# Value units 0 to 2 in the loop's common part, and one early projection instead of two

## The chip, the cores and the metric

The kernel runs on one core of one Trainium2 chip. The metric is the device time in microseconds (us); the median of several runs is quoted. The engines: TensorE does matmuls (PE in the profile; PEld is its weight load), VectorE is DVE, ScalarE is ACT, SyncE is SP and issues most of the loads.

## The reference, cut to what matters

One decoding step of a block: adaLN modulation, attention with a key and value cache, a squared-ReLU feed-forward part.

```python
B, Sq, D = 8, 1, 512;  Hq, Hkv, Sk, Dh = 32, 8, 8192, 128;  F = 1792
mod = (silu(c) @ w_mod)                       # six vectors sa, ca, ga, sb, cb, gb
h = layernorm(x) * (1 + ca) + sa
x = x + ga * A(h)      # q = h @ wq; p = softmax(q @ k_cache.T / sqrt(128)); o = p @ v_cache; o @ wo
h = layernorm(x) * (1 + cb) + sb
x = x + gb * B(h)      # relu(h @ w1 + b1)**2 @ w2 + b2
```

The two caches are 8 x 8 x 8192 x 128 bfloat16 values each, 134 MB. Each is read once. All else is about 15 MB.

## The kernel before

A batch is four key units and four value units. A unit is one load of 4 MB (two of the eight key-value heads), and four slots hold loaded units. The 64 units are loaded in order; the load of unit n + 4 waits until TensorE is done with unit n. The program of a batch is a hardware loop on TensorE, VectorE and ScalarE. Its body has a part "a" that all passes run, and a part "b" under a branch that the last pass skips. What only the last batch does stands after the loop ("post"). SyncE's program has no loop.

```python
def _looped(self, e, eng, passes):
    ...
    with nc.Fori(0, passes, engines=[pe], head_slot={pe: 0} if e == "tensor" else None) as i:
        for j, o in enumerate(self._part(e, (0, "a"))):
            self._emit(eng, o, first["a", j], seen)
        with eng.If(i < passes - 1):
            for j, o in enumerate(self._part(e, (0, "b"))):
                self._emit(eng, o, first["b", j], seen)
            ...                                  # wait for the counts, set the semaphores back
    for o in self._part(e, "post"):
        self._emit(eng, o, self._want(e, o, passes - 1), after)
```

The value units, with cuts (`...`). In the kernel before all four are in "b", and the last batch has its own copy of them after the loop:

```python
for b in range(B):
    lastb = b == B - 1
    Pg.at = (b, "a")
    ...                                          # keys: transposes, scores; softmax; pe_stream
    Pg.at = "post" if lastb else (b, "b")
    for p in range(NP):                          # value units 0..3
        if not lastu:
            for m in range(32):                  # 128 x 512 matmuls in four column groups
                ...                              # wait: this unit's load, the softmax
            osb = ...                            # VectorE copies 128 x 512 out of PSUM
            for i in range(4):                   # four SEL matmuls sum the groups;
                ...                              # the first of them releases the slot
            norm_last = ...                      # VectorE normalizes into oTn
            if lastb and p == 1:
                k_oP = early(0, 2, ...)          # gather: 16 matmuls and a copy
                ...                              # 14 bias matmuls (b1)
                project(0, 2, k_oP)              # 64 matmuls with wo
            if lastb and p == 2:
                k_oP = early(2, 3, [norm_last])
                ...                              # 4 bias matmuls (b2)
                project(2, 3, k_oP)              # 32 matmuls with wo
        else:                                    # the last unit of all, loaded in four chunks
            ...                                  # loads of B's weights w1 and w2 are issued
            for m in range(24): ...              # chunk 0 for m < 16, chunk 1 for the others
            direct(96, 112, 2, True, False)      # 16 narrow matmuls, chunk 2
            ...                                  # four SEL matmuls
            direct(112, 128, 3, False, True)     # 16 narrow matmuls, chunk 3
            ...                                  # normalize, the last 32 matmuls with wo
```

After the last value unit come the residual, the second layernorm, 56 matmuls with w1 and 56 with w2.

## Time and profile before

| | |
|---|---|
| time, median of 3 runs | 670.4 us (670.01 to 670.82) |
| bytes loaded | 283.65 MB, nearly all of it keys and values |
| TensorE, VectorE, ScalarE busy | 75%, 45%, 37% |
| DMA engines busy | 99.0% of 16 engines' span |

These lines are from the profile page of the kernel before: the span; the busy tenths of the DMA engines in 40 slices; one of the DMA queues with packets, MB and share (q8 carries instructions); and who stands in the chain of waits that ended last.

```profile
span 668.9 us, 16042 instructions
...
DMA  9999999999999999999999999999999999999996
...
q8 instruction: 11, 0.18, 0.1%
...
PE 54%; DMA 38%; DVE 3%; ACT 2%; SPq 2%; issue 1%
```

The DMA engines are busy 90% or more in 39 of 40 slices. The shares by engine of the last line are misleading on their own: where TensorE stands in the chain it is because it released a slot for a load that then waited in a queue (from issue to landing the 4 MB loads of keys and values took 33.6 and 27.8 us, where 4 MB at 431 GB/s are 9.7 us).

Windows of the kernel before: start and end, length, busy time of PE, PEld, DVE, ACT, POOL with instruction counts, then granted clock, DMA share, GB/s. First one batch's worth of the loop, then two of the last microseconds of loading.

```profile
553.00:631.00 78.00, 59.81 (x867) 41.43 (x866) 36.41 (x66) 29.74 (x36) 0.00 (x0) 0.87 1.00 431
...
663.00:664.00 1.00, 0.48 (x18) 0.48 (x19) 0.90 (x5) 0.00 (x0) 0.00 (x0) 0.50 0.14 55
664.00:665.00 1.00, 0.62 (x24) 0.53 (x21) 0.09 (x1) 0.00 (x0) 0.00 (x0) 0.50 0.07 29
```

In the loop the loads run at 431 to 432 GB/s with no gap, while TensorE is busy 60 of 78 us. (Six more such windows, from 85 us on, show the same.) At the end the share falls to 0.14, which is two of 16 engines, and 0.07, which is one: most DMA engines are done by about 662.5 us, but one or two are 1 to 2.5 us behind.

Timeline of TensorE in the last batch, kernel before (start, length, engine, line, what, and in brackets the idle time before it and what ended it):

```profile
643.04 1.78 PE L518 MATMUL PS<-oP,wo_sb 128*128 128x32 bf16 x64
645.20 1.91 PE L606 MATMUL PS<-ring,Pm 128*32 128x512 bf16 x32 [0.38 <-DMA ring<-in_A_v_cache_dram]
...
649.13 0.99 PE L518 MATMUL PS<-oP,wo_sb 128*128 128x32 bf16 x32 [0.19 <-DVE oP L512]
651.68 1.90 PE L665 MATMUL PS<-ring,Pm 128*32 128x512 bf16 x16 [1.56 <-DMA ring<-in_A_v_cache_dram]
...
664.92 1.01 PE L731 MATMUL PS<-hidT,ring 128*128 128x8 bf16 x24 [0.38 <-DMA ring<-in_B_w_dram]
```

64 projection matmuls (L518) while unit 2 is loading; unit 2 (L606) in 1.91 us at full clock (granted 1.00); 32 more projection matmuls; then the last unit's first 16 wide matmuls (L665), after a wait of 1.56 us for their chunk; at the end the w2 matmuls (L731), of which the last 24 wait 0.38 us for w2. The end of the chain of waits (start, length, what) says the same, a load of B's weights and then those matmuls:

```profile
649.87 15.01 DMA ring<-in_B_w_dram
...
664.92 0.59 PE PS L731 x16
```

### The profile page before, as it was taken

How to read it: one execution, taken by the hardware profiler on the slowest of the kernel's cores; microseconds unless marked ns; L12 is line 12 of the kernel's file. 1: busy time of each engine (PE TensorE's matmuls, PEld its weight loads, DVE VectorE, ACT ScalarE, POOL GpSimd, SP SyncE). 2: the span in 40 equal slices, each digit the busy share in tenths (PEclk: the TensorE clock that was granted, in tenths of full speed). 3: DMA queues.
4: the chain of work that ended last, by engine and by line, in shares of the span. 5: the costliest groups of instructions: out<-in, count | busy, mean ns of one | idle time of the engine just before them, and what ended most of it. 6: DMA issues, size and time to landing. Idle time of an engine off the chain costs nothing.

```text
span 668.9 us, 16042 instructions
## 1 busy us (share of the span) xinstructions
PE 501.8 (75%) x7348; PEld 347.5 (52%) x7348; DVE 301.2 (45%) x570; ACT 245.2 (37%) x289; POOL 17.8 (3%) x71
## 2 busy tenths in 40 slices
PE   3493974799539983699648996499836996399966
PEld 2382731676228751577317762287415773177644
DVE  1262741467216661367314672166503673156722
ACT  2151630466105650266304661066402653046600
POOL 7300000000000000000000000000000000000000
PEclk9696995799869996599957997699977999689995
DMA  9999999999999999999999999999999999999996
GB/s 373 436 402 435 421 429 435 433 431 427 437 433 433 425 433 435 433 429 429 435 431 435 427 433 435 431 425 433 435 433 431 427 437 433 431 427 433 435 410 246
DMA packets 12962, 283.88 MB, mean 424 GB/s; under 512 B 1266, under 2 KB 2323, under 8 KB 4372
## 3 DMA queue, kind: packets, MB, share of 16 engines
q1 hardware_dynamic: 12900, 283.65, 99.0%
q8 instruction: 11, 0.18, 0.1%
q10 hardware_dynamic: 48, 0.02, 0.0%
q14 instruction: 3, 0.02, 0.0%
HBM read 283.66 MB, written 0.01 MB: 424 GB/s over the span
## 4 chain that ended last, share of the span: by engine, by line
PE 54%; DMA 38%; DVE 3%; ACT 2%; SPq 2%; issue 1%
PE PS L467 36%; DMA ring<-in_A_k_cache_dram 36%; PE PS L484 9%; PE PS L564 3%; PE PS L606 2%; DMA ring<-in_B_w_dram 2%; PE PS L458 1%; SPq L648 1%; ACT KTb L472 1%; ACT P_sb L554 1%; DVE m L491 1%; DVE O_sb L612 1%; PE PS L585 0%; DVE Dm L545 0%; PE PS L616 0%
## 5 line engine op out<-in xcount | busy, mean ns | idle before, releaser
L472 ACT ACTIVATE KTb<-PS 128x1024 bf16<-128x1024 bf16 x192 | 196.7, 1024 | 344.3 <-PE PS L467 344.3
L467 PE MATMUL PS<-IDENT,ring 128*128 128x128 bf16 x4096 | 268.1, 228 | 51.3 <-DMA ring<-in_A_k_cache_dram 51.3
L467 PEld LDWEIGHTS PS<-IDENT,ring 128*128 128x128 bf16 x4096 | 247.5, 102 | 99.8 <-DMA ring<-in_A_k_cache_dram 52.9
L474 DVE COPY KTb<-PS 128x1024 bf16<-128x1024 bf16 x320 | 210.1, 688 | 145.1 <-PE PS L467 143.0
L606 PE MATMUL PS<-ring,Pm 128*32 128x512 bf16 x992 | 81.1, 485 | 61.9 <-DMA ring<-in_A_v_cache_dram 61.0
L612 DVE CAST O_sb<-PS 128x512 bf16<-128x512 f32 x31 | 21.4, 692 | 138.8 <-PE PS L606 138.8
L484 PE MATMUL PS<-KTb,Qb 128*32 128x512 bf16 x1024 | 78.8, 385 | 4.5 <-ACT KTb L472 4.5
L606 PEld LDWEIGHTS PS<-ring,Pm 128*32 128x32 bf16 x992 | 28.9, 115 | 99.3 <-DMA ring<-in_A_v_cache_dram 62.4
L458 PE MATMUL PS<-IDENT 128*128 128x512 bf16 x120 | 31.3, 380 | 0.0
L554 ACT ACTIVATE P_sb<-PS,negm 128x512 bf16<-128x512 f32 x32 | 21.6, 686 | 20.2 <-DVE negm L550 20.2
L616 PEld LDWEIGHTS PS<-SEL,O_sb 128*128 128x128 bf16 x124 | 5.3, 99 | 44.9 <-DVE O_sb L612 44.9
L616 PE MATMUL PS<-SEL,O_sb 128*128 128x8 bf16 x124 | 8.0, 170 | 24.8 <-DVE O_sb L612 24.8
L484 PEld LDWEIGHTS PS<-KTb,Qb 128*32 128x32 bf16 x1024 | 15.4, 94 | 21.1 <-ACT KTb L472 8.5
L579 DVE COPY Pm<-PS 64x512 bf16<-64x512 bf16 x48 | 19.5, 419 | 13.3 <-PE PS L564 12.3
L491 DVE TENSOR_REDUCE m<-PS 128x1 f32<-128x512 f32 x32 | 22.1, 689 | 6.6 <-PE PS L484 6.6
L564 PEld LDWEIGHTS PS<-IDENT,P_sb 128*64 128x64 bf16 x512 | 21.9, 109 | 5.2 <-ACT P_sb L554 5.2
L564 PE MATMUL PS<-IDENT,P_sb 128*64 128x128 bf16 x512 | 23.2, 222 | 1.2 <-ACT P_sb L554 1.2
L458 PEld LDWEIGHTS PS<-IDENT 128*128 128x128 bf16 x120 | 9.9, 103 | 10.8 <-issue 3.4
L623 DVE TENSOR_TENSOR oTn<-PS,rinv 128x8 f32 (+1 forms) x31 | 6.0, 194 | 14.0 <-PE PS L616 14.0
L472 ACT ACT_TABLE_LOAD x8 | 10.3, 1283 | 3.2 <-issue 3.2
L576 ACT ACTIVATE Pm<-PS 64x512 bf16<-64x512 bf16 x16 | 9.5, 592 | 3.1 <-PE PS L564 2.5
L393 PE MATMUL PS<-ring,KTb 128*32 128x512 bf16 x56 | 7.2, 627 | 3.6 <-DMA ring<-in_A_wq_dram 3.5
(126 smaller groups left out, 102.2 us busy)
## 6 DMA issues: line engine op xcount, KB each, us to landing
ring<-in_A_k_cache_dram SPq DMA_DIRECT2D x32, 4096.0 KB, 33.6
ring<-in_A_v_cache_dram SPq DMA_DIRECT2D x31, 4096.0 KB, 27.8
ring<-in_A_wq_dram SPq DMA_DIRECT2D x1, 4096.0 KB, 19.9
ring<-in_w_mod_dram SPq DMA_DIRECT2D x1, 3072.0 KB, 10.4
wo_sb<-in_A_wo_dram SPq DMA_DIRECT2D x1, 3072.0 KB, 46.1
ring<-in_A_v_cache_dram SPq DMA_DIRECT2D x1, 2048.0 KB, 24.2
ring<-in_B_w_dram SPq DMA_DIRECT2D x3, 512.0 KB, 18.4
ring<-in_B_w_dram SPq DMA_DIRECT2D x1, 1344.0 KB, 21.0
```

The costliest lines, as they stand in the source:

```text
L458: op("tensor", lambda e: e.matmul(bank(at).rearrange("p (a r) -> p a r", a=4), IDENT[:, :], rhs))
L467: t = op("tensor", lambda e, j=j, i=i: e.matmul(STG[j][:, i, :], src[:, 32 * k + 8 * j + i, :], IDENT[:, :], is_transpose=True), [loaded[n ...
L472: stg_free[j] = op("scalar", lambda e, j=j, dst=dst: e.activation(dst, STG[j], ACT.Copy), [t])
L474: stg_free[j] = op("vector", lambda e, j=j, dst=dst: e.tensor_copy(dst, STG[j]), [t])
L484: t = op("tensor", lambda e, hf=hf, q=q, rhs=rhs: e.matmul(PS[32 * q:32 * (q + 1), k, :], Qb[:, 2 * p + hf, :], rhs, start=(p == 0 and hf ...
L491: return op("vector", lambda e: e.tensor_reduce(m4[:, k:k + 1], bank(k), AX.X, ALU.max), [t])
L554: exps.append(op("scalar", lambda e, k=k: e.activation(P_sb[:, k, :], bank(k), ACT.Exp, bias=negm[:, 0:1], scale=inv_sqrt, accum_out=rs4[: ...
L564: t = op("tensor", lambda e, k=k, i=i, hf=hf, src=src: e.matmul(STG[k][64 * hf:64 * (hf + 1), i, :], src, IDENT[:, :], is_transpose=True, ...
L579: done.append(op("vector", lambda e, dst=dst, frm=frm: e.tensor_copy(dst, frm), [t, k_pm]))
L606: t = op("tensor", lambda e, p=p, m=m, cg=cg, vt=vt, Obank=Obank: e.matmul(Obank[32 * cg:32 * (cg + 1), :], lhs[:, p, 32 * m:32 * m + 32], ...
L612: t = op("vector", lambda e, osb=osb, Obank=Obank: e.tensor_copy(osb, Obank), [t])
L616: t = op("tensor", lambda e, i=i, osb=osb, oT_ps=oT_ps: e.matmul(oT_ps, osb[:, i * 128:(i + 1) * 128], SEL[:, i, :], start=(i == 0), stop= ...
```

## The change

Read from the diff, the intent is shorter code: units 0 to 2 of every batch move into the common part "a", so the last batch runs them in the loop and their second copy after the loop goes away. Only unit 3 stays under the branch. Since nothing of the last batch alone can stand in part "a", the early projection of the last batch, which was in two parts (after units 1 and 2), is done once after unit 2; the 14 b1 matmuls move in between the 16th and the 17th of unit 3's 24 wide matmuls. The program becomes shorter: counted in the compiled program, with two instructions for each matmul (weight load and matmul; the page of before counts 7348 of each), TensorE's code after the loop shrinks from 947 to 698 instructions, and the loop itself stays at 1747.

```diff
--- before.py
+++ after.py
@@ -500,19 +500,18 @@
         hT_ps = [bank(i)[:, 0:16 * 7].rearrange("p (f a b) -> p f a b", f=7, a=2) for i in range(2)]
         yT_ps = bank(2)[:, 0:KT * B].rearrange("p (k b) -> p k b", k=KT)
 
-        def early(q0, q1, deps):
-            nq = q1 - q0
-            pP = bank(6)[:, 64 * q0:64 * q1].rearrange("p (j g b) -> p j g b", j=4, g=2 * nq)
+        def early(deps):
+            pP = bank(6)[:, 0:192].rearrange("p (j g b) -> p j g b", j=4, g=6)
             for hl in range(REP):
                 for j in range(4):
                     t = op("tensor", lambda e, hl=hl, j=j: e.matmul(
                         pP[32 * hl:32 * (hl + 1), j, :, :].rearrange("p (q h) b -> p h q b", h=2),
-                        PERM[:, j, :], oTn_p[:, :, q0:q1, hl, :], start=True, stop=True,
+                        PERM[:, j, :], oTn_p[:, :, 0:3, hl, :], start=True, stop=True,
                         tile_position=(0, 32 * hl)), deps)
-            return op("vector", lambda e: e.tensor_copy(oP[:, :, 2 * q0:2 * q1, :], pP), [t])
-
-        def project(q0, q1, k_oP):
-            for g in range(2 * q0, 2 * q1):
+            return op("vector", lambda e: e.tensor_copy(oP[:], pP), [t])
+
+        def project(k_oP):
+            for g in range(6):
                 for j in range(4):
                     for k in range(KT):
                         op("tensor", lambda e, g=g, j=j, k=k: e.matmul(
@@ -594,8 +593,9 @@
             lhs = Pm[:, :, :, :].rearrange("p u t r -> p u (t r)")
             rinv_p = rinv[:].rearrange("p (h q r) -> p h q r", h=2, q=NP)
             oTn_p = oTn[:].rearrange("p (h q r) b -> p h q r b", h=2, q=NP)
-            Pg.at = "post" if lastb else (b, "b")
             for p in range(NP):
+                if p == NP - 1:
+                    Pg.at = "post" if lastb else (b, "b")
                 n = 2 * NP * b + NP + p
                 vt = tiles(n % NSLOT)
                 Obank = bank(p)
@@ -623,20 +623,13 @@
                     s_bank_free[p] = norm_last = op("vector", lambda e, p=p, b=b, oT_ps=oT_ps: e.tensor_tensor(
                         oTn_p[:, :, p, :, Pg.index(b)].rearrange("p h r o -> p h (r o)"), oT_ps.rearrange("p (h r) -> p h r", h=2), rinv_p[:, :, p, :], ALU.mult),
                         [t])
-                    if lastb and p == 1:
-                        k_oP = early(0, 2, [norm_last, k_all] + stg_free + hold)
-                        for f in range(FT):
-                            op("tensor", lambda e, f=f: e.matmul(
-                                hT_ps[f // 7][:, f % 7, 1, :], fcol(b1_row[:], f), ONE8[:, :],
-                                start=(f % 7 == 0), stop=False, skip_group_check=True), [d_b2, s_bank_free[f // 7]])
-                        project(0, 2, k_oP)
-                    if lastb and p == 2:
-                        k_oP = early(2, 3, [norm_last])
+                    if lastb and p == NP - 2:
+                        Pg.at = "post"
+                        project(early([norm_last, k_all] + stg_free + hold))
                         for k in range(KT):
                             op("tensor", lambda e, k=k: e.matmul(
                                 yT_ps[:, k, :], b2_row[:, k * 128:(k + 1) * 128], ONE8[:, :],
-                                start=(k == 0), stop=False, skip_group_check=True), [s_bank_free[2]])
-                        project(2, 3, k_oP)
+                                start=(k == 0), stop=False, skip_group_check=True), [d_b2, s_bank_free[2]])
                 else:
 
                     s0 = (n + 1) % NSLOT
@@ -667,6 +660,11 @@
                             vt[:, 4 * m:4 * m + 4, :], start=(m < 4), stop=(m >= 20),
                             tile_position=(0, 32 * cg)),
                             [loaded[n][0 if m < 16 else 1], k_rinv] + pmd[m // 8])
+                        if m == 15:
+                            for f in range(FT):
+                                op("tensor", lambda e, f=f: e.matmul(
+                                    hT_ps[f // 7][:, f % 7, 1, :], fcol(b1_row[:], f), ONE8[:, :],
+                                    start=(f % 7 == 0), stop=False, skip_group_check=True), [d_b2, s_bank_free[f // 7]])
                     osb = O_sb[:, 1, :]
                     t = op("vector", lambda e: e.tensor_copy(osb, bank(3)), [t])
                     direct(96, 112, 2, True, False)
```

## The prediction

> **What bounds the kernel now.** The DMA queue. Page part 2: the 16 DMA engines are 90% busy or more in 39 of 40 slices. In seven windows of 78 us (one batch each, from 85 to 631 us) the DMA share is 1.00 at 431 to 432 GB/s, while TensorE is busy about 60 of 78 us. The list of waits has TensorE standing 61.0 us (L606) and 51.3 us (L467) until loads land; issue to landing, 28 to 34 us (page part 6), is about three 4 MB loads of 9.7 us, so one is always queued. Nothing a compute engine does in the loop is on the critical path unless it delays a slot's release by more than about 18 us (estimate from that).

> **Inside the loop the change only moves the branch** from before value unit 0 to between units 2 and 3. There TensorE waits 5.0 to 5.6 us for unit 3 anyway (timeline). Loads, releases and instruction mix are unchanged. Expected: nothing.

> **The last batch changes.** Before (timeline, 636 to 669 us): units 0 and 1 end at 642.0; an early gather, 14 bias matmuls and 64 projection matmuls (1.78 us) fill the wait; unit 2 lands at 645.2 and runs at full clock (1.91 us); gather, 32 more projection matmuls (0.99 us) end at 650.1; unit 3's first chunk lands at 651.7. After: TensorE idles about 3 us from 642.0. After such a gap unit 2 took 3.02 to 3.60 us in batches 0 to 6, at granted clock 0.5. [...]
> Estimate: unit 2 ends near 648.5; copy 0.69, SEL 0.26, normalization 0.19; gather and copy about 0.8; 96 projection matmuls at 28 ns = 2.7 us; so TensorE is free at about 653.4, 1.7 us after unit 3's first chunk. Then 16 matmuls (1.9 us), 14 bias matmuls (0.6), 8 matmuls (1.04), partly using up waits of 0.68 and 0.36 us. Attention's last normalization moves from 657.4 to about 658.7 (+1.3 us; only +0.2 if unit 2 stays at full clock).

> **How much reaches the end.** The chain of waits ends in the load of B's second weight (landing at 664.9), not in attention. TensorE waits 0.42 us for the first weight at 660.1 and 0.38 us for the second at 664.9: slack of about 0.6 us. So +1.3 becomes about +0.6; +0.2 becomes 0.

> **Predicted: 670.9 us (before 670.4), 8 in 10 between 669.4 and 672.4.** Faster by over 2%: 0.005; within 2%: 0.985; slower: 0.01.

> **What would show it.** Loop windows: still 1.00 DMA share, about 431 GB/s. Timeline of the last batch: unit 2 after an idle gap of about 3 us, lasting 3.0 to 3.6 us; 96 projection matmuls in one run of about 2.7 us; unit 3's first matmul released by TensorE's own order, near 653.5, no longer by the load; bias matmuls between its 16th and 17th. End: the wait for the second weight shrinks or is gone.

> **What would make it wrong.** A stall at the jump out of the loop, now just ahead of the gather with only about 0.5 us to hide it ([...]this trace shows none at the old place). Another landing of the second weight, whose last packets straggle.

## The result, and the profile after

| | median us | runs |
|---|---|---|
| before | 670.2 | 4 (669.80 to 670.82) |
| after | 670.46 | 4 (669.77 to 670.78) |

The ratio is 1.0002, 95% interval 0.9984 to 1.0019: the same. A ratio here is the mean time of one kernel's runs over the mean of the other's of the same rounds, so it isn't quite the ratio of the medians. 670.46 us lies in the predicted range, 0.4 us from the predicted 670.9.

The page after, the same lines:

```profile
span 667.9 us, 16012 instructions
...
DMA  9999999999999999999999999999999999999996
...
q8 instruction: 10, 0.16, 0.1%
...
PE 54%; DMA 40%; DVE 3%; ACT 2%; issue 1%; SPq 0%; DVEq 0%
```

The windows after, the same stretches:

```profile
553.00:631.00 78.00, 59.95 (x867) 41.31 (x867) 36.41 (x66) 29.74 (x36) 0.00 (x0) 0.89 1.00 432
...
663.00:664.00 1.00, 0.86 (x32) 0.87 (x33) 0.64 (x4) 0.00 (x0) 0.00 (x0) 0.50 0.13 39
664.00:665.00 1.00, 0.93 (x30) 0.78 (x27) 0.03 (x1) 0.00 (x0) 0.00 (x0) 0.50 0.01 2
```

The loop is unchanged: share 1.00, 432 GB/s. At the end next to nothing is left between 664 and 665 us (0.01 of 16 engines, before 0.07). One 16 KB instruction load is gone (q8: 10 instead of 11).

TensorE's timeline of the last batch after:

```profile
644.74 2.70 PE L606 MATMUL PS<-ring,Pm 128*32 128x512 bf16 x32 [3.34 <-DMA ring<-in_A_v_cache_dram]
...
649.79 2.74 PE L517 MATMUL PS<-oP,wo_sb 128*128 128x32 bf16 x96 [0.51 <-DVE oP L511]
...
652.65 1.05 PE L658 MATMUL PS<-ring,Pm 128*32 128x512 bf16 x16
653.63 0.61 PE L665 MATMUL PS<-ONE,b_row 1*128 1x8 bf16 x14
654.16 0.40 PE L658 MATMUL PS<-ring,Pm 128*32 128x512 bf16 x3
655.20 0.59 PE L658 MATMUL PS<-ring,Pm 128*32 128x512 bf16 x5 [0.64 <-issue]
...
663.14 1.79 PE L729 MATMUL PS<-hidT,ring 128*128 128x8 bf16 x56 [0.97 <-DVE hidT L725]
```

- Unit 2 (L606 at 644.74) follows an idle wait of 3.34 us and takes 2.70 us (mean granted clock 0.68).
- The 96 projection matmuls (L517) are one run of 2.74 us.
- Unit 3's first matmul (L658 at 652.65) no longer waits for its load; it follows TensorE's own work. It runs at full clock: 16 matmuls in 1.05 us (granted 1.00), where before they took 1.90 (granted 0.50).
- Between the 19th and the 20th of unit 3's matmuls there is a pause of 0.64 us for which the profile names no releaser.
- The w2 matmuls (L729) show as one run of 56, but this view begins a new line only after an idle time of 0.15 us. w2 is loaded in four pieces, for 16, 16, 16 and 8 of these matmuls. In the trace's list of landings the last piece is there at 664.50 us, while the matmuls run, and the last 8 waited about 0.1 us for it: the 56 took 1.79 us, and 1.66 where nothing held them (after_again, below).

So the chain of waits, as the profile draws it, no longer passes through the load of w2, though the two end within 0.1 us of each other. It leaves the loads when unit 2 lands (the first of these two lines of the chain of waits ends at 644.70 us), and is TensorE's and VectorE's from then on, up to the w2 matmuls:

```profile
617.14 27.56 DMA ring<-in_A_v_cache_dram
...
663.14 1.80 PE PS L729 x56
```

The span of this one profile is 1.0 us shorter than that of before (667.9 and 668.9), but the times of the four runs don't differ. A second profile of each kernel was needed before any of this could be read.

### The profile page after: what moved, and what is told of

It reads as the page before. It is cut to its first block, busy times and chain, and to the rows that moved or that the text cites. A ratio compares the mean times of both kernels' runs of the same rounds, so it can differ in the third digit from the quotient of the medians.

```text
span 667.9 us, 16012 instructions
## 1 busy us (share of the span) xinstructions
PE 499.2 (75%) x7332; PEld 346.1 (52%) x7332; DVE 301.0 (45%) x569; ACT 245.1 (37%) x289; POOL 17.5 (3%) x71
## 4 chain that ended last, share of the span: by engine, by line
PE 54%; DMA 40%; DVE 3%; ACT 2%; issue 1%; SPq 0%; DVEq 0%
DMA ring<-in_A_k_cache_dram 36%; PE PS L467 35%; PE PS L484 9%; DMA ring<-in_A_v_cache_dram 4%; PE PS L563 3%; PE PS L606 2%; PE PS L458 1%; ACT KTb L472 1%; DVE O_sb L612 1%; ACT P_sb L553 1%; DVE m L491 1%; PE PS L517 0%; PE PS L584 0%; PE PS L658 0%; PE PS L729 0%
## 5 line engine op out<-in xcount | busy, mean ns | idle before, releaser
L467 PE MATMUL PS<-IDENT,ring 128*128 128x128 bf16 x4096 | 266.9, 228 | 51.3 <-DMA ring<-in_A_k_cache_dram 51.3
L467 PEld LDWEIGHTS PS<-IDENT,ring 128*128 128x128 bf16 x4096 | 246.2, 102 | 99.6 <-DMA ring<-in_A_k_cache_dram 52.5
L606 PE MATMUL PS<-ring,Pm 128*32 128x512 bf16 x992 | 82.2, 490 | 65.5 <-DMA ring<-in_A_v_cache_dram 64.6
L606 PEld LDWEIGHTS PS<-ring,Pm 128*32 128x32 bf16 x992 | 29.3, 115 | 103.4 <-DMA ring<-in_A_v_cache_dram 66.0
L484 PEld LDWEIGHTS PS<-KTb,Qb 128*32 128x32 bf16 x1024 | 15.5, 94 | 21.1 <-ACT KTb L472 8.5
L623 DVE TENSOR_TENSOR oTn<-PS,rinv 128x8 f32 x31 | 6.0, 194 | 14.3 <-PE PS L616 14.3
```

Source lines behind the costliest of these rows:

```text
L467: t = op("tensor", lambda e, j=j, i=i: e.matmul(STG[j][:, i, :], src[:, 32 * k + 8 * j + i, :], IDENT[:, :], is_transpose=True), [loaded[n ...
L484: t = op("tensor", lambda e, hf=hf, q=q, rhs=rhs: e.matmul(PS[32 * q:32 * (q + 1), k, :], Qb[:, 2 * p + hf, :], rhs, start=(p == 0 and hf ...
L606: t = op("tensor", lambda e, p=p, m=m, cg=cg, vt=vt, Obank=Obank: e.matmul(Obank[32 * cg:32 * (cg + 1), :], lhs[:, p, 32 * m:32 * m + 32], ...
```

## The experiments

My theory: the loads bound the kernel; in the loop the moved branch is hidden; in the last batch TensorE has a little slack against the load of w2, which swallows most of what its longer chain costs. First rival: the loop gains and the late projection loses, and the two cancel. Second rival: TensorE's chain bounds the end, and its work shows in full. Two more questions came from the profile: is the pause of 0.64 us a wait for instructions, and why did w2 land earlier in this profile?

| kernel | median us | ratio to before (95%) | span of its profile, us | last data packet ends at, us | TensorE instruction loads from 636 to 662 us |
|---|---|---|---|---|---|
| before | 670.2 | | 668.9 | 665.1 | 3 |
| before_again | 670.6 (1 run, state unknown) | | 668.8 | 664.9 | 3 |
| after | 670.46 | 1.0002 (0.9984 to 1.0019) | 667.9 | 664.1 | 2 |
| after_again | 670.65 | 1.0006 (0.9992 to 1.0019) | 669.0 | 664.1 | 2 |
| loop_only | 669.97 | 0.9997 (0.9983 to 1.0010) | 668.8 | 664.9 | 3 |
| tail_only | 670.43 | 1.0002 (0.9988 to 1.0015) | 668.8 | 664.9 | 3 |
| tail_pad | 670.42 | 1.0000 (0.9987 to 1.0014) | 668.2 | 664.3 | 4 |
| no_project | 670.2 | 0.9998 (0.9984 to 1.0011) | 668.0 | 664.1 | 2 (one at 661.9) |
| slack12 | 672.31 | 1.0027 (1.0013 to 1.0040) | 670.5 | 664.0 | 2 |
| bias_first | 670.3 | 0.9997 (0.9983 to 1.0011) | 669.5 | 664.1 | 2 |
| warm | 670.0 | 0.9996 (0.9982 to 1.0010) | 668.0 | 664.2 | 2 |
| warm_bias | 670.53 | 1.0003 (0.9990 to 1.0017) | 668.7 | 664.0 | 2 |
| delay4 | 670.15 | 0.9998 (0.9985 to 1.0012) | 668.5 | 664.7 | 3 |
| delay14 | 798.38 | 1.1903 (1.1877 to 1.1928) | 796.1 | | |

The last two columns are read from the list of DMA packets in each trace. An instruction load is one 16 KB packet of queue q8; that it holds 256 instructions is shown further down. Each ratio is to the runs of before in the same session (medians 670.12, 670.25 and 670.29 us for the sessions after the first). All results passed the comparison with the reference, even that of no_project, which leaves out most of a sum: presumably the part it leaves out is too small against x for the comparison to notice.

One more reading of the traces helps with all that follows. From the landing of w2's last piece to the end of the span it is 3.43 us in ten of the fourteen profiles, after among them: there the last 8 matmuls start as soon as that piece has landed. In the other four (after_again, slack12, bias_first, warm_bias) it is 4.3 to 6.2 us: there TensorE came later by its own chain. In these four the last w2 matmul starts 1.48 to 1.49 us after the first. What it takes beyond that elsewhere is TensorE's slack against w2: 0.75 us in before, 0.79 in before_again, 0.56 in tail_only, 0.40 in warm, 0.38 in tail_pad, 1.6 in loop_only and no_project, 0.8 in delay4 and delay14, and 0.13 in after. (A landing is noted some 0.4 us after the load's last data packet ended.)

### before_again: the kernel before, a second profile

No edit.

> The kernel before, unchanged, for a second profile. Both theories: 669.8 to 670.8 us. Theory (the end waits for the loads, the tensor engine has slack): in the last batch unit 2 at full clock (about 1.9 us), and the chain of waits again ends in a load of B's second weight, which lands 19 to 20.5 us after value unit 2 landed. If that landing moves by more than 0.3 us between two profiles of the same kernel, the 0.5 us by which the profiled run of after had a shorter tail than that of before is such scatter and not a gain.

Measured: 670.6 us. TensorE's timeline (unit 2, the last w2 matmuls):

```profile
645.03 3.25 PE L606 MATMUL PS<-ring,Pm 128*32 128x512 bf16 x32 [1.27 <-DMA ring<-in_A_v_cache_dram]
...
664.74 1.01 PE L731 MATMUL PS<-hidT,ring 128*128 128x8 bf16 x24 [0.42 <-DMA ring<-in_B_w_dram]
```

Unit 2 took 3.25 us here, not 1.91, with the projection in front of it as before. In this trace the granted clock stepped to 0.5 at 644.4 us; in the first profile it held at 1.0 until 649.8 us. This part of my expectation was wrong: the full clock of unit 2 in the first profile was where the clock's steps happened to fall, not a property of the kernel. The rest held: the chain ends in the load of w2 again (the last 24 w2 matmuls wait 0.42 us for it), and the last data packet moved by 0.2 us only (665.1 and 664.9). Two profiles don't give the scatter of that landing, though. The 27 other runs of before whose spans are on record are all shorter than these two: 667.8 to 668.7 us, against 668.9 and 668.8. By the 3.43 us above, w2's last piece had landed by 664.4 to 665.3 us in them; in the two profiles it landed at 665.5 and 665.3.

### after_again: the changed kernel, a second profile and five timed runs

No edit.

> The changed kernel, unchanged, for a second profile and for the time. Both: ratio 0.998 to 1.002. A pause of 0.64 us stands in the profile of after between the 19th and the 20th of unit 3's 24 matmuls, where no semaphore is waited for. Theory of fetch (the tensor engine's next 256 instructions were not there yet): the pause is again at the same instruction, 0.2 to 1.5 us long, and an instruction load begins 1 to 4 us before its end. Rival (scatter, a hidden wait for a load): no pause, or at another place.

Measured: ratio 1.0006 (0.9992 to 1.0019).

```profile
644.91 3.60 PE L606 MATMUL PS<-ring,Pm 128*32 128x512 bf16 x32 [4.25 <-DMA ring<-in_A_v_cache_dram]
...
655.47 0.40 PE L658 MATMUL PS<-ring,Pm 128*32 128x512 bf16 x3
656.37 0.59 PE L658 MATMUL PS<-ring,Pm 128*32 128x512 bf16 x5 [0.51 <-issue]
...
664.32 1.66 PE L729 MATMUL PS<-hidT,ring 128*128 128x8 bf16 x56 [0.97 <-DVE hidT L725]
```

The pause is again between the 19th and the 20th matmul (L658, 3 matmuls, then 0.51 us, then 5). An instruction load began at 653.85 us in the packet list and TensorE went on at 656.37, 2.5 us later; in the first profile after these were 652.78 and 655.20, 2.4 us. Unit 2 took 3.60 us this time, so TensorE's chain was 1.0 us longer than in the first profile: from unit 2's start to the last normalization 13.5 us here, 12.5 there, 12.2 and 12.1 in the two profiles of before. That is nearly the whole of the 1.1 us between the spans 667.9 and 669.0. The w2 matmuls (L729) waited for nothing here: the last piece landed at 664.53 us, 1.1 us before its 8 matmuls began. The shorter span of the first profile was luck with the clock.

### loop_only: only the loop's side of the change

Units 0 and 1 go into the common part, the early projection stays as before.

```diff
-            Pg.at = "post" if lastb else (b, "b")
             for p in range(NP):
+                if p == 2:
+                    Pg.at = "post" if lastb else (b, "b")
 ...
                     if lastb and p == 1:
+                        Pg.at = "post"
                         k_oP = early(0, 2, [norm_last, k_all] + stg_free + hold)
```

> Units 0 and 1 of every batch in the loop's common part, unit 2 and 3 not; the early projection in two parts as before. Theory (the loop's side is worth nothing): ratio to before 0.998 to 1.002, the last batch's unit 2 at full clock (about 1.9 us) since 64 projection matmuls fill the wait before it. Rival (the move of the branch gains in the loop and the late projection gives it back): 0.995 or less, with TensorE's waits for value loads shorter in batches 0 to 6.

Measured: ratio 0.9997 (0.9983 to 1.0010).

```profile
645.04 1.91 PE L607 MATMUL PS<-ring,Pm 128*32 128x512 bf16 x32 [0.22 <-DMA ring<-in_A_v_cache_dram]
...
664.79 1.00 PE L733 MATMUL PS<-hidT,ring 128*128 128x8 bf16 x24 [0.67 <-DMA ring<-in_B_w_dram]
```

Unit 2 took 1.91 us, as at granted clock 1.00 in before (which, after before_again, may be chance), and the end waits 0.67 us for w2. The move of the branch is worth nothing that can be measured. The rival of cancelling needed 0.995 and falls. (Unit 2 isn't moved here. But after and tail_only, next, differ by the move of all three units alone, and both measured 1.0002.)

### tail_only: only the last batch's side of the change

The early projection once, between units 2 and 3, and b1 as after, but all value units in "b" and "post" as before.

```diff
+            Pg.at = "post" if lastb else (b, "b")
             for p in range(NP):
-                if p == NP - 1:
-                    Pg.at = "post" if lastb else (b, "b")
 ...
                     if lastb and p == NP - 2:
-                        Pg.at = "post"
                         project(early([norm_last, k_all] + stg_free + hold))
```

> All of the last batch's value units after the loop as before, the early projection once, between units 2 and 3, as after. Theory: ratio 0.998 to 1.002; TensorE idle about 3 us before unit 2, which lasts 2.5 to 3.6 us; unit 3's first matmul 0.7 to 2 us after its load landed. Rival of cancelling: 1.002 to 1.006. Theory of fetch: no pause at the 20th matmul of unit 3, because the 256-instruction edge there has moved (by 217 instructions) into the projection[...]; a later edge lies in the matmuls after unit 3's copy and may show a pause. If the pause is still between the 19th and 20th, fetch is wrong.

Measured: ratio 1.0002 (0.9988 to 1.0015), against the rival's 1.002 to 1.006.

```profile
656.08 0.54 PE L649 MATMUL PS<-Pm,ring 128*128 128x32 bf16 x15
656.83 0.19 PE L649 MATMUL PS<-Pm,ring 128*128 128x32 bf16 x1 [0.21 <-issue]
...
664.75 1.01 PE L727 MATMUL PS<-hidT,ring 128*128 128x8 bf16 x24 [0.19 <-DMA ring<-in_B_w_dram]
```

Unit 2 took 3.33 us after an idle wait of 4.05 us, and TensorE's chain to the last normalization was 12.6 us long. Still the last 24 w2 matmuls waited, by 0.19 us: TensorE had slack left against w2's landing, 0.56 us by the count above. The pause isn't at the 20th matmul of unit 3 any more. It stands, 0.21 us long, between the 15th and the 16th narrow matmul (L649). In the compiled program of this kernel an edge of 256 instructions lies there, within one instruction; its block's load began at 654.43 us, 2.4 us before TensorE went on at 656.83.

### tail_pad: as tail_only, with 256 instructions more

```diff
+                if lastb and p == 2:
+                    for _ in range(128):
+                        op("tensor", lambda e: e.matmul(bank(7)[:, 0:8], IDENT[:, :], IDENT[:, 0:8]))
```

> As tail_only, with 128 tiny matmuls (256 instructions, about 28 ns each) in the wait of about 4 us before the last batch's unit 2. Theory of the instruction load: each 16 KB block of TensorE's instructions occupies one of the 16 DMA engines for 1.1 us; what that engine owes of B's second weight lands that much later. Instruction loads between 636 and 662 us: before, before_again, tail_only, loop_only 3 each, and the last data packet ended at 664.9 to 665.1 us; after, after_again 2, and it ended at 664.1. Here 4 are expected, the last data packet at 665.6 to 666.1, the end 0.7 to 1.2 us later than tail_only (ratio to before 1.001 to 1.002). Rival (the landing scatters, or follows the tensor engine's own timing): last packet at 664.9 or earlier.

Measured: ratio 1.0000 (0.9987 to 1.0014), four instruction loads, but the last data packet at 664.3 us and not at 665.6 or later. My theory, in the form that each instruction load adds 1.1 us to w2's landing, falls, and the rival that I had named, that the landing scatters, stands. The windows show what else happened (compare 0.14 and 0.07 in the same two windows before):

```profile
663.00:664.00 1.00, 0.81 (x30) 0.82 (x31) 0.69 (x4) 0.00 (x0) 0.00 (x0) 0.50 0.25 94
664.00:665.00 1.00, 0.94 (x29) 0.78 (x27) 0.00 (x0) 0.00 (x0) 0.00 (x0) 0.50 0.02 8
```

Between 663 and 664 us four engines' worth of work was left (0.25 of 16), nearly twice as much as before, and after 664 almost none. That fits instruction loads that fell on different engines, each late by about one load, where in before one engine would have had two. The trace has no engine numbers, so this is only argued.

Two more things in this trace bear on other questions. First, the 256 instructions move the edge by one whole block, back to where it was in tail_only, and the pause is there again: the 16th narrow matmul starts 0.25 us after the 15th, where the others follow at 0.025 us, and the block's load began at 653.68 us, 2.6 us before that. (By the profile's own reckoning the idle time is 0.07 us, too short for the view.) Second, the tiny matmuls fill the wait ahead of unit 2 from 640.41 to 643.75 us, all but 0.78 us of it, and still the granted clock fell to 0.5 at 644.2 us and unit 2 took 3.41 us.

### no_project: the changed kernel without 92 of the 96 projection matmuls (wrong)

```diff
         def project(k_oP):
-            for g in range(6):
-                for j in range(4):
+            for g in range(1):
+                for j in range(1):
```

> The changed kernel with 4 of its 96 early projection matmuls (wrong result, on purpose): 2.6 us less work for TensorE in the last batch and 184 instructions fewer. Theory (the end waits for loads): unit 3 waits for its loads again, and the time falls by no more than 1.2 us (ratio 0.998 to 1.000), not by 2.6. Instruction loads from 636 to 662 us: 1 or 2; with 1 the last data packet ends at 662.8 to 663.4 us. Rival (TensorE's chain bounds the end): 2 us or more less, 0.997 or below.

Measured: ratio 0.9998 (0.9984 to 1.0011); the rival needed 0.997 or below.

```profile
650.32 0.29 PE L517 MATMUL PS<-oP,wo_sb 128*128 128x32 bf16 x4 [0.51 <-DVE oP L511]
...
661.69 1.02 PE L729 MATMUL PS<-hidT,ring 128*128 128x8 bf16 x32 [0.98 <-DVE hidT L725]
663.16 0.59 PE L729 MATMUL PS<-hidT,ring 128*128 128x8 bf16 x16 [0.45 <-DMA ring<-in_B_w_dram]
664.57 0.37 PE L729 MATMUL PS<-hidT,ring 128*128 128x8 bf16 x8 [0.83 <-DMA ring<-in_B_w_dram]
```

TensorE had 2.5 us less to do between units 2 and 3 (4 matmuls in 0.29 us at L517, not 96 in 2.74). It reached the w2 matmuls at 661.69 us, 1.5 and 2.6 us sooner than in the two profiles of after (663.14 and 664.32), and gave that back in two waits for w2, 0.45 and 0.83 us, where the profiles of after have at most 0.1 us. The last data packet ended at 664.1 us with one instruction load before 661 us and a second at 661.9, not at the 662.8 to 663.4 us that one load would have given.

### slack12: the changed kernel with 12 dummy matmuls after the projection

```diff
                         project(early([norm_last, k_all] + stg_free + hold))
+                        pe_stream(12, 7)
```

> The changed kernel with 12 dummy matmuls of 512 columns (2.6 us at full clock) after the early projection. In after and after_again the end followed TensorE's chain with the loads already there, so theory: all of it but 0 to 0.5 us reaches the end: 2.1 to 3.5 us longer than after, ratio to before 1.003 to 1.005. Rival (still 0.6 us or more of slack): below 1.003. Theory of fetch: the pause moves from the 20th matmul of unit 3 to the sixth of the 14 bias matmuls, which is where the 256-instruction edge then stands.

Measured: ratio 1.0027 (1.0013 to 1.0040), about 1.9 us longer than the changed kernel (672.31 and 670.46 us). It is just below the 1.003 that I had put as the lower limit of my theory, so by what I had written down the rival (0.6 us or more of slack left) held; the interval reaches to both sides of that line.

```profile
652.71 3.54 PE L458 MATMUL PS<-IDENT 128*128 128x512 bf16 x12
...
657.34 0.61 PE L666 MATMUL PS<-ONE,b_row 1*128 1x8 bf16 x14
```

The dummies took 3.54 us, more than the 2.6 I had reckoned and than the 2.75 us of the same 12 in warm, below; that the clock was at 0.5 for part of them is my estimate from these two times. There is no pause at all, neither at the sixth of the 14 bias matmuls (L666, all 14 in 0.61 us) nor elsewhere in unit 3: the block's load began at 653.04 us and was needed only after 657 us. So the pause itself, 0.5 to 0.6 us, was won back. TensorE's chain from unit 2 to the last normalization is 15.5 us, 2.4 more than the mean of the two profiles of after (12.5 and 13.5). The w2 matmuls didn't wait here, and there by 0.1 us at most, so the profiles show hardly any reserve; the time alone, with an interval of 0.9 to 2.7 us against before, doesn't tell 2.4 us from a somewhat smaller cost. I had named a new place for the pause without checking that TensorE would get there before the load.

### bias_first: the changed kernel with the bias matmuls in VectorE's waits

```diff
-                        project(early([norm_last, k_all] + stg_free + hold))
+                        for f in range(FT):
+                            ...                       # the 14 b1 matmuls, from unit 3 to here
+                        k_oP = early([norm_last, k_all] + stg_free + hold)
                         for k in range(KT):
                             ...                       # the 4 b2 matmuls
+                        project(k_oP)
```

> The changed kernel with the 14 bias matmuls ahead of the gather and the 4 ahead of the projection, in waits for the vector engine. Theory: unit 3's copy starts 0.4 to 0.9 us earlier after unit 2's end than in after; the pause is still at the 20th matmul of unit 3 (same edge), shorter or equal; 2 instruction loads, last data packet again at 664.1. The end then falls by 0 to 0.7 us against after, within the noise of the times: ratio to before 0.998 to 1.001.

Measured: ratio 0.9997 (0.9983 to 1.0011).

```profile
649.98 0.60 PE L629 MATMUL PS<-ONE,b_row 1*128 1x8 bf16 x14 [0.23 <-issue]
...
654.08 2.32 PE L663 MATMUL PS<-ring,Pm 128*32 128x512 bf16 x19
656.71 0.82 PE L663 MATMUL PS<-ring,Pm 128*32 128x512 bf16 x5 [0.31 <-issue]
```

The pause is where the edge is, at the 20th matmul, now 0.31 us. Unit 3's matmuls came later, not 0.4 to 0.9 us earlier: in this trace the clock stood at 0.5 from 643.6 to 657.2 us, and the first 19 took 2.32 us. (The profile is of its slowest run, 671.38 us; the other four took 669.8 to 670.5.) The first of these lines shows the jump out of the loop laid bare: TensorE is idle for 0.23 us before the first instruction after the loop, with nothing to wait for. In the changed kernel this lies inside a wait for VectorE.

### warm: the changed kernel with 12 dummy matmuls between units 1 and 2

```diff
             for p in range(NP):
+                if p == 2:
+                    pe_stream(12, 4)
                 if p == NP - 1:
                     Pg.at = "post" if lastb else (b, "b")
```

> The changed kernel with 12 dummy matmuls of 512 columns between units 1 and 2 of every batch (2.6 us at full clock, in a wait of about 3.3 us). Theory: the last batch's unit 2 takes 1.9 to 2.2 us instead of 2.70 and 3.60 in the two profiles of after, so the half clock there came from the idle wait; the last normalization stands 0.5 to 1.6 us earlier after unit 2's landing. The end falls at most to where the second weight's landing (last packet about 664.1 us) lets it: 0 to 0.9 us, ratio to before 0.998 to 1.000. The pause, if any, at the sixth of the 14 bias matmuls, where the edge now stands. The 84 dummies in batches 0 to 6 cost nothing.

Measured: ratio 0.9996 (0.9982 to 1.0010).

```profile
644.80 1.91 PE L608 MATMUL PS<-ring,Pm 128*32 128x512 bf16 x32 [0.57 <-DMA ring<-in_A_v_cache_dram]
...
654.51 0.41 PE L667 MATMUL PS<-ONE,b_row 1*128 1x8 bf16 x9 [0.86 <-issue]
...
662.94 2.06 PE L731 MATMUL PS<-hidT,ring 128*128 128x8 bf16 x56 [0.97 <-DVE hidT L727]
```

Unit 2 took 1.91 us (2.70 and 3.60 in the profiles of after), and not by chance: it did so in all eight batches of this trace and of that of warm_bias, where batches 0 to 6 of the two profiles of after took 2.8 to 3.6. So its slowness came from the wait ahead of it. What counts isn't idleness alone: the dummies here are 512 columns wide, and tail_pad's, with 8 columns, filled the wait and didn't help. The 12 dummies (2.75 us) lengthen the loop by 24 instructions and so shift the edge back by 24: it lies at the sixth of the 14 bias matmuls, and there the pause is, 0.86 us, after five of them. TensorE's chain to the last normalization is 12.2 us, but the pause took back most of what the clock had given. The end waits for w2 again: its 56 matmuls (L731) took 2.06 us and not 1.66, in two waits too short for the view.

### warm_bias: bias_first and warm together

> bias_first and warm together: the candidate to beat both kernels. Theory: TensorE's chain is shortest here, the last 24 matmuls of B's second half wait for the load again, and the time is 669.3 to 670.2 us, ratio to before 0.998 to 1.000; a gain of 0.1% that the times can't tell from none. Rival (TensorE's chain is what sets the time): 0.9975 or below.

Measured: ratio 1.0003 (0.9990 to 1.0017), 670.53 us. It doesn't beat either kernel.

```profile
652.11 1.04 PE L665 MATMUL PS<-ring,Pm 128*32 128x512 bf16 x7
654.38 2.29 PE L665 MATMUL PS<-ring,Pm 128*32 128x512 bf16 x17 [1.23 <-issue]
...
664.03 1.66 PE L731 MATMUL PS<-hidT,ring 128*128 128x8 bf16 x56 [0.98 <-DVE hidT L727]
```

The pause has grown to 1.23 us, between the seventh and the eighth matmul of unit 3, once more at the edge. TensorE got there sooner, and the block came no sooner: its load began at 651.83 us (651.99 in warm), and TensorE went on at 654.38 (654.51). The w2 matmuls didn't wait for w2, and TensorE's chain to the last normalization, 13.2 us, wasn't the shortest (warm 12.2), both against what I expected.

### delay4 and delay14: how much slack a release has in the loop

The kernel before, with vector reductions nobody uses ahead of value unit 0 in batches 0 to 6: 4 of them, or 14.

```diff
+                if p == 0 and not lastb:
+                    for i in range(4):              # 14 in delay14
+                        k_rinv = op("vector", lambda e, i=i: e.tensor_reduce(
+                            dly[:, i:i + 1], P_sb[:, :, :].rearrange("p a n -> p (a n)"), AX.X, ALU.max))
                 n = 2 * NP * b + NP + p
```

> The kernel before with four useless vector reductions (about 2.1 us each) ahead of value unit 0 in batches 0 to 6, not in the last: every batch's first two value units, and with them two releases of load slots, come about 8.6 us later. Theory (about 18 us of slack on these releases): no change, ratio 0.998 to 1.002, DMA share still 1.00 in the loop. Rival (release times of the value units matter to the loop): 1.01 or more (7 batches x 1 us or more).

> The same with 14 reductions, about 30 us per batch in batches 0 to 6. Theory: 18 us are hidden, the other 8 to 14 us per batch are not: 60 to 100 us longer in all, ratio 1.09 to 1.15, and the DMA share falls below 0.95 in the loop. If it is under 1.03 the slack is larger than I reckoned; over 1.2 it is smaller.

Measured: delay4 0.9998 (0.9985 to 1.0012), with the DMA share at 1.00 or 1.01 in each of six windows of 78 us in the loop. One reduction took 2.26 us (my 2.1 was an estimate; a reduction over 512 columns, a quarter of these, took 0.69 us in before), and four of them held value unit 0 up by 8.7 us in each of the seven batches, all of it hidden. delay14: 1.1903 (1.1877 to 1.1928), 128 us longer, which is 18.3 us in each of 7 batches and more than the 1.09 to 1.15 that I expected. One stretch of one batch as a window, and the matmuls of value unit 0 with the wait before them:

```profile
395.00:415.00 20.00, 3.67 (x40) 1.45 (x44) 16.07 (x9) 0.00 (x0) 0.00 (x0) 0.53 0.18 79
```

```profile
410.53 3.44 PE L611 MATMUL PS<-ring,Pm 128*32 128x512 bf16 x32 [30.76 <-DVE dly L602]
```

Value unit 0 was held up for 30.76 us; the loads then ran dry for most of the 20 us from 395 us (share 0.18). Of 30.8 us, 18.3 were not hidden, so the slack of these releases is about 12.5 us and not the 18 us I had estimated.

## Why the prediction was right, point by point

- **The loads bound the kernel: shown.** In no_project 2.5 us less work for TensorE, and in delay4 a delay of 8.7 us in each of seven batches, left the time as it was. The DMA share in the loop's windows of 78 us is 1.00 or 1.01 in before, before_again, after, after_again and delay4; in delay14 it fell to 0.18 for 20 us.
- **In the loop the change is worth nothing: shown.** loop_only 0.9997; after and tail_only, which differ by the move alone, both 1.0002. The slack that I gave as 18 us is about 12.5 us (delay14); the conclusion didn't hang on it.
- **Unit 2 after the idle wait takes 3.0 to 3.6 us: nearly.** 2.70 and 3.60 in the two profiles after, 3.33 in tail_only. warm and tail_pad show the reason: with wide matmuls in the wait it takes 1.91 us, with none, or with tiny ones (3.41 us), it doesn't. It isn't a matter of long gaps alone: in before_again the clock fell to 0.5 at 644.4 us, after 3.4 us in which TensorE was busy for about 2.6 us, with matmuls of 8 to 32 columns only, and no gap was longer than 1.3 us; in tail_pad it fell at 644.2 us, after 3.4 us of which matmuls of 8 columns filled about 3.0. As to when it steps, all 36 stretches in the clock record of before, and all 42 in that of after, begin a multiple of 3.41 us after the first; the rule behind the steps isn't shown. What I missed is that the steps are not tied to the kernel's course: the one in the last batch came 4.6 us after unit 2's start in before and 0.6 us ahead of it in before_again, so unit 2 of the kernel before was at full clock in one profile (1.91 us) and took 3.25 us in the other. The 1.3 us which I charged to the change was in part chance on both sides.
- **Unit 3 at half clock: wrong.** I took over the 1.90 us of before for its first 16 matmuls. After the projection, with no wait in between, they took 1.05 and 1.26 us, 0.6 to 0.8 us less (in after the granted clock went back to 1.0 at 652.55 us; in tail_only, also with no wait, they took 1.73 us).
- **A stall at the jump: not there, but close by.** The jump costs about 0.25 us (bias_first 0.23, warm_bias 0.25). The stall I read as a wait for the next block of instructions. What the traces show of it: the instruction queue moves packets of 16 KB; TensorE's program, shorter by 249 instructions, makes one such load less (q8: 10 in after, 11 in before); tail_pad's 256 more instructions make one load more than in tail_only (4 and 3 from 636 to 662 us) and leave the pause at the same matmul, so I count 256 instructions to a block; the loop of 1747 instructions makes no instruction load after its first pass (none from 100.5 to 640.8 us in before); and the pause is, within one instruction, at the edge 2048 (8 x 256) instructions behind the loop's head in after, after_again, bias_first, warm and warm_bias, one block further on in tail_only, and two in tail_pad. In each of these seven profiles the load of that block began 2.4 to 2.6 us before TensorE went on; the transfer itself took 1.1 us of that (1.11 in after). In slack12 the load began 4 us or more before the block was needed, and there was no pause. When a block is asked for, the traces don't show. The pause was 0.2 to 1.2 us long (tail_only 0.21, warm_bias 1.23). In the kernel before the value units with their waits lay between these edges; in the changed kernel the projection lies there, whose 96 matmuls run through 192 instructions in 2.74 us.
- **How much reaches the end: the right size, in part by luck.** In TensorE's chain two errors nearly cancel: unit 3's first 16 matmuls were 0.6 to 0.8 us faster than I took them to be, and the pause, which wasn't in my sum, cost 0.5 to 0.6 us. The chain to the last normalization became 0.3 to 1.4 us longer (12.5 and 13.5 us, after 12.2 and 12.1), where I had 1.3. Its slack against w2 was 0.75 and 0.79 us before, where I had 0.6. And I had w2 land when it did before. In all seven profiles with the change's short code after the loop (after, after_again, no_project, slack12, bias_first, warm, warm_bias) the last data packet ended at 664.0 to 664.2 us, against 664.7 to 665.1 in before, before_again, loop_only, tail_only and delay4. Of the two profiles of after, one still ends with w2 (slack 0.13 us), the other with TensorE's chain. The time sits where it was within 0.2%. The predicted +0.5 us can be neither confirmed nor refuted: 0.9984 to 1.0019 is -1.1 to +1.3 us, and "no change" would have been as good a guess.
- **Why w2 lands earlier: open, and most of it may be scatter.** While an instruction load runs, 1.0 to 1.1 us, mostly 15 and not 16 data packets are in flight in the traces (before: 15 during the loads at 640.79 and 647.16 us, 16 ahead of them), so it does take one DMA engine away. The kernels with a late landing have three such loads between 636 and 662 us, those with an early one at most two. But tail_pad, with four, landed at 664.3 us. The number of instruction loads alone doesn't decide it. Whether two of them fall on the same engine may; the traces don't tell. The runs without a kept trace speak for scatter. Four of loop_only's five runs, with the same three loads in their code, had spans of 667.9 to 668.2 us, so w2's last piece landed by 664.5 to 664.8 us in them, not at 665.4 us as in its profile. The mean span of before is 668.3 us (27 runs), those of no_project and warm 668.1. If w2 ends these runs, as it does in the profiles of all three, it lands earlier by about 0.2 us on average, not by the 0.5 to 1.1 us that lie between the profiles.

The first rival (gain and loss cancel between loop and tail) falls with loop_only and tail_only, both at 1.000. The second (TensorE's chain bounds the end) doesn't fit before, whose two profiles end with w2 and leave TensorE 0.75 and 0.79 us of slack (no run took work away from before itself), and is half true for after: work added there shows (slack12), work removed doesn't (no_project).

## What to carry to other kernels

When the loads run without a gap, ask only what changes for the last load, and for the work behind it; moving code about inside the loop was free here, where the releases have about 12.5 us of slack. At the end of this kernel two chains finish within a microsecond of each other, so shortening one hands the end to the other: look for the second-latest chain before working on the latest. A single profile was off by 1 us here through where the clock's steps fell alone (after and after_again: unit 2 in 2.70 and 3.60 us), so take two before explaining a difference of that size, and hold them against the spans of the runs that weren't profiled; and a pause with no releaser in straight-line code just behind a loop is worth holding against the instruction loads in the packet list (here it lay at the 256-instruction edges, in seven profiles).
